# A Fourier filter on half the spectrum, folded a second time: quarter-length transforms and a batch build spread over the FFN

## The chip, the cores and the metric

The kernel runs on one core of one Trainium2 chip. The number that counts is device time in microseconds (us) of one execution. Engines of the core work side by side, each through its own list of instructions in a fixed order: TensorE (PE, with its weight loads shown apart as PEld), VectorE (DVE), ScalarE (ACT), GpSimd (POOL, which here starts the loads) and SyncE (SP, which starts the stores). TensorE's clock has two levels, 1.2 and 2.4 GHz; a profile shows the share of the upper one that was granted.

## The reference

Two parts, one after the other. For each of 8 batches of 3008 positions by 256 channels a real Fourier transform along the positions, a product with a complex filter (1505 frequencies by 256 channels), and the inverse transform. Then, on the 24064 rows that come out, a gated feed-forward network (FFN):

```python
X = np.fft.rfft(x, axis=1)                       # x: 8 x 3008 x 256
y = np.fft.irfft(X * (filt_r + 1j*filt_i)[None], n=3008, axis=1)
x = y.reshape(24064, 256)
out = (np.maximum(x @ w_gate, 0.0) * (x @ w_val)) @ w_out   # 256 -> 1536 -> 256
```

## The kernel before

The transforms are matrix products. A real transform of 3008 positions needs cosines and sines of 3008 x 1505 angles; the kernel first folds position n with position 3008-n, so that sum and difference of 1505 positions remain, and one square table each of cosines (`G_c`) and sines (`G_s`), 1505 x 1505 in 16 bits, serves forward and inverse.

Stages:

- `build_uv(b)` (L255 on) makes the folded input of a batch in 12 chunks of up to 128 positions: POOL loads the chunk `xa` and its mirror `xm` (L265, L269), PE reverses the mirror with a permutation matrix (`xrev`, L271), ACT copies it out of PSUM (L278), DVE writes sum and difference into `uv` (L279, L281).
- `gen_acs` and `gen_stripe` make the tables in six column stripes of 256. Stripe 0 comes from angles on DVE and `Sin` on ACT (L185 to L208); the others from stripe 0 by a rotation on PE: DVE builds three diagonal matrices `dg` (L217), four products of 256 columns go into `gen_s` and `gen_c`, ACT copies them out (L230, L231).
- `forward_chunk` makes 128 frequencies: 12 products of 256 columns into `xr_ps` (L299), 12 into `xi_ps` (L306); ACT scales both out of PSUM (L313, L315); six operations of DVE multiply by the filter into `yf` (L318 to L324).
- `inverse_batch` makes, per half of the channels (2) and per tile of 512, 512 and 481 positions, 12 products into `p_ps` (L338) and 12 into `q_ps` (L345); ACT copies `q_ps` (L352), DVE writes p-q and p+q to the two mirrored places of `y` (L353, L359).
- `ffn_batch` goes through 8 windows of 384 positions (the last has 320). Per window 12 blocks of gate and value, four products each (`g_ps` L376, `v_ps` L383), a copy on ACT (`ge`, L389) and the gated product on DVE (`h`, L390); then 36 products into `o_ps` (L398), a copy and a store.

All PSUM tiles come from one pool of eight banks used in turn. Two batches are built ahead of everything else (`n_pre` = 2); the tables are made stripe by stripe, and after each stripe both batches' forward chunks of those columns run. From then on, in the order of the program: for batch b the forward transform (if b is 2 or more), the build of batch b+2, the inverse, the FFN:

```python
        nb = b + n_pre
        if nb < B:
            uv_tiles[nb] = build_uv(nb)
        y = inverse_batch(b, yf_tiles.pop(b))
        ffn_batch(b, y)
```

A framework orders each engine's list when the program is built (`tc.high_priority()` moves a block forward) and adds the semaphore waits; when the kernel runs, each engine takes its list strictly in turn.

Of the kernel before, what the change touches and what calls it, by code (L numbers as in the profile page):

```python
# [19 lines left out]
def kernel(  # L20
# [10 lines left out]
    nc = tc.nc  # L31
# [4 lines left out]
    NF = S // 2 + 1  # L36
    Dff = moe_w_gate.shape[1]
# [36 lines left out]
    xload = ctx.enter_context(tc.tile_pool(name="xload", bufs=3))  # L74
# [20 lines left out]
    nc.vector.tensor_add(wvec, wvec, wvec_tmp)
    nc.vector.tensor_scalar(out=wvec, in0=wvec, scalar1=-1.0 / N, scalar2=2.0 / N,
                            op0=ALU.mult, op1=ALU.add)
    wvec_neg = const.tile([P, nM], FP32)
    nc.vector.tensor_scalar_mul(wvec_neg, wvec, -1.0)

    lastc = nM - 1
    rows_last = msz(lastc)
    hi_last = rows_last - 1 if (lastc * P + rows_last - 1) == NF - 1 else rows_last
    cond_last = hi_last - 1
# [6 lines left out]
                            op0=ALU.is_equal)  # L111
    if cond_last != P - 1:
# [13 lines left out]
    G_c = gmat.tile([P, nM, NF], FP16)  # L126
    G_s = gmat.tile([P, nM, NF], FP16)

    MAGIC = float(2 ** 23)
    two_pi = 2.0 * math.pi  # L130

    nDer = nGW - 1
    if nDer > 0:
        acs = const.tile([P, nM, nDer, 3], FP32)

    def gen_acs():
        if nDer == 0:
            return
        colk = gen.tile([P, nDer], FP32, tag="colk", bufs=1)
        nc.gpsimd.iota(colk, [[GW, nDer]], base=GW, channel_multiplier=0,  # L140
                       allow_small_or_imprecise_dtypes=True)
        for mi in range(nM):
            rows = msz(mi)
            ph = gen.tile([P, 2, nDer], FP32, tag="acs_ph")
            nc.vector.tensor_scalar(
                out=ph[:rows, 0, :], in0=colk[:rows, :],
                scalar1=rowval_n[:rows, mi:mi + 1], scalar2=None, op0=ALU.mult)
            nc.vector.tensor_scalar(
                out=ph[:rows, 1, :], in0=ph[:rows, 0, :],
                scalar1=0.25, scalar2=None, op0=ALU.add)  # L150
            rnd = gen.tile([P, 2, nDer], FP32, tag="acs_rn")
            nc.vector.tensor_scalar(
                out=rnd[:rows, 0, :], in0=ph[:rows, 0, :],
                scalar1=MAGIC, scalar2=MAGIC, op0=ALU.add, op1=ALU.subtract)
            nc.vector.tensor_scalar(
                out=rnd[:rows, 1, :], in0=ph[:rows, 1, :],
                scalar1=MAGIC, scalar2=MAGIC, op0=ALU.add, op1=ALU.subtract)
            red = gen.tile([P, 2, nDer], FP32, tag="acs_rd")
            nc.vector.scalar_tensor_tensor(
                out=red[:rows, 0, :], in0=rnd[:rows, 0, :], scalar=-1.0,  # L160
                in1=ph[:rows, 0, :], op0=ALU.mult, op1=ALU.add)
            nc.vector.scalar_tensor_tensor(
                out=red[:rows, 1, :], in0=rnd[:rows, 1, :], scalar=-1.0,
                in1=ph[:rows, 1, :], op0=ALU.mult, op1=ALU.add)
            nc.scalar.activation(
                out=acs[:rows, mi, :, 1], in_=red[:rows, 0, :],
                func=AF.Sin, scale=two_pi)
            nc.scalar.activation(
                out=acs[:rows, mi, :, 0], in_=red[:rows, 1, :],
                func=AF.Sin, scale=two_pi)  # L170
            nc.vector.tensor_scalar(
                out=acs[:rows, mi, :, 2], in0=acs[:rows, mi, :, 1],
                scalar1=-1.0, scalar2=None, op0=ALU.mult)

    def gen_stripe(gj):
        cols = gwsz(gj)
        c0 = gj * GW
        if gj == 0:
            colv = gen.tile([P, GW], FP32, tag="colv", bufs=1)
            nc.gpsimd.iota(colv[:, :cols], [[1, cols]], base=c0, channel_multiplier=0,  # L180
                           allow_small_or_imprecise_dtypes=True)
            for mi in range(nM):
                rows = msz(mi)
                phi = gen.tile([P, 2, GW], FP32, tag="phi", bufs=1)
                nc.vector.tensor_scalar(  # L185
                    out=phi[:rows, 0, :cols], in0=colv[:rows, :cols],
                    scalar1=rowval_n[:rows, mi:mi + 1], scalar2=None, op0=ALU.mult)
                nc.vector.tensor_scalar(
                    out=phi[:rows, 1, :cols], in0=phi[:rows, 0, :cols],
                    scalar1=0.25, scalar2=None, op0=ALU.add)  # L190
# [48 lines left out]
    def load_weights():  # L239
# [230 lines left out]
```

## Time and profile before

| what | value |
|---|---|
| time, median of 4 runs (lowest to highest) | 1445.79 us (1443.77 to 1448.33) |
| the profiled execution's own time | 1445.38 us |
| its span in the profile | 1443.6 us |
| PE busy | 1319.0 us, 91% of the span, 9168 products |
| DVE, ACT, POOL busy | 49%, 43%, 9% |
| mean granted clock | 0.975 |

The span runs from the first to the last instruction that the profile shows; the other 1.8 us of that execution lie around it. "Busy" of DVE and ACT adds up durations, and neighbouring instructions overlap, so what an instruction occupies is read from the distance of two starts in the timeline. The chain of waits names, going back from the last instruction, what each step waited for; its PE pieces give the rate at which products really follow each other.

### The profile page before, as it was taken

How to read it: one execution, taken by the hardware profiler on the slowest of the kernel's cores; microseconds unless marked ns; L12 is line 12 of the kernel's file. 1: busy time of each engine (PE TensorE's matmuls, PEld its weight loads, DVE VectorE, ACT ScalarE, POOL GpSimd, SP SyncE). 2: the span in 40 equal slices, each digit the busy share in tenths (PEclk: the TensorE clock that was granted, in tenths of full speed). 3: DMA queues.
4: the chain of work that ended last, by engine and by line, in shares of the span. 5: the costliest groups of instructions: out<-in, count | busy, mean ns of one | idle time of the engine just before them, and what ended most of it. 6: DMA issues, size and time to landing. Idle time of an engine off the chain costs nothing.

```text
span 1443.6 us, 24775 instructions
## 1 busy us (share of the span) xinstructions
PE 1319.0 (91%) x9168; PEld 897.8 (62%) x9168; DVE 707.8 (49%) x1977; ACT 626.7 (43%) x1466; POOL 124.4 (9%) x241
## 2 busy tenths in 40 slices
PE   2179989988999799997999899997999999999999
PEld 0047736663677557784577746775577856776666
DVE  2486635552554435543455525554355435553455
ACT  2255524551554225542355315542255415542455
POOL 6700030012000300003000120002000000000000
PEclk9999989998999899998999989998999999999999
DMA  8700030122010301103011120102011000100011
GB/s 115 91 1 1 1 43 23 34 45 31 25 35 29 44 0 34 37 18 43 12 37 38 16 30 26 38 26 32 1 34 37 19 1 26 35 27 1 19 35 35
DMA packets 60248, 42.46 MB, mean 29 GB/s; under 512 B 6942, under 2 KB 59616, under 8 KB 60128
## 3 DMA queue, kind: packets, MB, share of 16 engines
q0 software_dynamic: 32992, 16.24, 9.4%
q1 hardware_dynamic: 27136, 24.65, 5.1%
q8 instruction: 71, 1.16, 0.3%
q14 instruction: 49, 0.40, 0.1%
HBM read 32.44 MB, written 24.64 MB: 40 GB/s over the span
## 4 chain that ended last, share of the span: by engine, by line
PE 63%; issue 29%; POOL 4%; DMA 3%; DVE 1%; ACT 0%; POOLq 0%; DVEq 0%; ACTq 0%
PE o_ps L398 13%; PE g_ps L376 13%; PE v_ps L383 13%; PE p_ps L338 7%; PE q_ps L345 6%; PE xr_ps L299 5%; PE xi_ps L306 5%; DMA xm<-in_x_dram 2%; POOL xm L269 2%; POOL xa L265 1%; DMA xa<-in_x_dram 1%; POOL filt_r_sb L251 0%; POOL w_out_sb L246 0%; POOL filt_i_sb L251 0%; PE xrev L271 0%
## 5 line engine op out<-in xcount | busy, mean ns | idle before, releaser
L390 DVE SCALAR_TENSOR_TENSOR h<-ge,v_ps 128x384 f16<-128x384 f16 (+1 forms) x768 | 409.9, 545 | 290.5 <-ACT ge L389 199.4
L389 ACT CAST ge<-g_ps 128x384 f16<-128x384 f32 (+1 forms) x768 | 360.0, 472 | 110.0 <-PE g_ps L376 78.1
L376 PE MATMUL g_ps<-y,w_gate_sb 128*128 128x384 f16 (+1 forms) x1536 | 370.2, 323 | 0.0
L383 PE MATMUL v_ps<-y,w_val_sb 128*128 128x384 f16 (+1 forms) x1536 | 370.2, 323 | 0.0
L398 PE MATMUL o_ps<-w_out_sb,h 128*128 128x256 f16 (+1 forms) x2304 | 263.0, 273 | 0.0
L398 PEld LDWEIGHTS <-h 128*128 128x128 f16 (+1 forms) x2304 | 225.8, 98 | 33.2 <-issue 1.7
L383 PEld LDWEIGHTS <-w_val_sb 128*128 128x128 f16 x1536 | 150.2, 98 | 94.2
L376 PEld LDWEIGHTS <-w_gate_sb 128*128 128x128 f16 x1536 | 150.3, 98 | 89.3
L299 PE MATMUL xr_ps<-uv,G_c 128*128 128x256 f16 (+3 forms) x1152 | 145.0, 274 | 26.7 <-ACT G_c L208 26.7
L404 ACT COPY ob<-o_ps 128x256 f32<-128x256 f32 x192 | 71.4, 372 | 204.6 <-PE o_ps L398 185.7
L306 PE MATMUL xi_ps<-uv,G_s 128*128 128x256 f16 (+3 forms) x1152 | 146.4, 274 | 5.9 <-ACT G_s L205 5.9
L338 PE MATMUL p_ps<-G_c,yf 128*128 128x512 f16 (+1 forms) x576 | 141.5, 398 | 0.0
L299 PEld LDWEIGHTS <-G_c 128*128 128x128 f16 (+3 forms) x1152 | 113.2, 100 | 41.8 <-ACT G_c L208 27.2
L345 PE MATMUL q_ps<-G_s,yf 128*128 128x512 f16 (+1 forms) x576 | 130.3, 375 | 0.0
L353 DVE TENSOR_TENSOR y<-p_ps,qs 128x512 f16<-128x512 f32 (+1 forms) x48 | 32.7, 682 | 196.3 <-ACT qs L352 196.3
L269 POOL DMA_DIRECT2D xm<-in_x_dram x96 | 52.8, 562 | 869.2 <-PE xrev L271 865.7
L352 ACT CAST qs<-q_ps 128x512 f16<-128x512 f32 (+1 forms) x48 | 27.7, 578 | 229.7 <-PE q_ps L345 229.7
L306 PEld LDWEIGHTS <-G_s 128*128 128x128 f16 (+3 forms) x1152 | 113.6, 100 | 21.5 <-ACT G_s L205 9.1
L338 PEld LDWEIGHTS <-yf 128*128 128x128 f16 x576 | 59.3, 103 | 73.1 <-issue 12.3
L345 PEld LDWEIGHTS <-yf 128*128 128x128 f16 x576 | 56.1, 97 | 67.0 <-issue 1.1
L271 PE MATMUL xrev<-xm,J_mid 128*128 128x256 f16 (+1 forms) x88 | 28.7, 352 | 75.1 <-DMA xm<-in_x_dram 74.1
L313 ACT ACTIVATE xt<-xr_ps,wvec 128x256 f16<-128x256 f32 x96 | 45.3, 473 | 82.8 <-PE xr_ps L299 77.0
(68 smaller groups left out, 650.2 us busy)
## 6 DMA issues: line engine op xcount, KB each, us to landing
out_dram<-ob SPq DMA_DIRECT2D x184, 128.0 KB, 1.7
xa<-in_x_dram POOLq DMA_DIRECT2D x88, 64.0 KB, 2.5
xm<-in_x_dram POOLq DMA_DIRECT2D x80, 64.0 KB, 2.5
w_gate_sb<-in_moe_w_gate_dram POOLq DMA_DIRECT2D x2, 384.0 KB, 6.5
w_val_sb<-in_moe_w_val_dram POOLq DMA_DIRECT2D x2, 384.0 KB, 5.7
w_out_sb<-in_moe_w_out_dram POOLq DMA_DIRECT2D x12, 64.0 KB, 2.7
filt_r_sb<-in_filt_r_dram POOLq DMA_DIRECT2D x11, 64.0 KB, 3.1
filt_i_sb<-in_filt_i_dram POOLq DMA_DIRECT2D x11, 64.0 KB, 3.3
```

Source lines behind the costliest of these rows:

```text
L269: nc.gpsimd.dma_start(xm16[:R, :], x[b, r0:r0 + R, :])
L299: nc.tensor.matmul(xr_ps[:F, :D], lhsT=G_c[:rows, sc, f0:f0 + F], rhs=uv[:rows, sc, 0, :], start=(sc == 0), stop=(sc == nM - 1))
L306: nc.tensor.matmul(xi_ps[:F, :D], lhsT=G_s[:rows, sc, f0:f0 + F], rhs=uv[:rows, sc, 1, :], start=(sc == 0), stop=(sc == nM - 1))
L313: nc.scalar.activation(out=xt[:F, 0, :], in_=xr_ps[:F, :D], func=AF.Copy, scale=wvec[:F, fc:fc + 1])
L338: nc.tensor.matmul(p_ps[:dn, :L], lhsT=yf[:F, fc, 0, d0:d0 + dn], rhs=G_c[:F, fc, t0:t0 + L], start=(fc == 0), stop=(fc == nM - 1))
L345: nc.tensor.matmul(q_ps[:dn, :L], lhsT=yf[:F, fc, 1, d0:d0 + dn], rhs=G_s[:F, fc, t0:t0 + L], start=(fc == 0), stop=(fc == nM - 1))
L376: nc.tensor.matmul(g_ps[:Fn, :L], lhsT=w_gate_sb[:dn, dc, fc * P:fc * P + Fn], rhs=y[:dn, dc, t0:t0 + L], start=(dc == 0), stop=(dc == nDC ...
L383: nc.tensor.matmul(v_ps[:Fn, :L], lhsT=w_val_sb[:dn, dc, fc * P:fc * P + Fn], rhs=y[:dn, dc, t0:t0 + L], start=(dc == 0), stop=(dc == nDC ...
L389: nc.scalar.copy(ge[:Fn, :L], g_ps[:Fn, :L])
L390: nc.vector.scalar_tensor_tensor(out=h[:Fn, fc, :L], in0=ge[:Fn, :L], scalar=0.0, in1=v_ps[:Fn, :L], op0=ALU.max, op1=ALU.mult)
L398: nc.tensor.matmul(o_ps[:gn, :D], lhsT=h[:Fn, fc, g0:g0 + gn], rhs=w_out_sb[:Fn, fc, :], start=(fc == 0), stop=(fc == nFF - 1))
L404: nc.scalar.copy(ob[:gn, :], o_ps[:gn, :D])
```

## The change

The input is folded twice. Positions n, 3008-n, 1504+n and 1504-n are combined, so that even and odd frequencies part: 753 even and 752 odd ones, each over 753 positions. Four components per position stand in `uv`. Three pairs of tables replace the one: `G2` (even frequencies, both directions, 753 x 753), `AoF` (odd, forward) and `AoI` (odd, inverse), each in three column stripes in place of six, from 18 angle blocks and 36 rotated blocks (before 12 and 60).

- `build_uv`: 6 chunks; per chunk four loads, two reversals, and eight operations of DVE, four of which read the reversal in PSUM (the copy on ACT goes). For the first two batches the angles of `G2` and `AoF` stripe 0 are made inside it. The pool of its buffers goes from three to two.
- `forward_chunk`: 12 chunks as before, each with 6+6 products in place of 12+12. What ACT and DVE do per chunk is the same.
- `inverse_batch`: tiles of 512 and 241 positions; 4 x 6 products per tile; two copies on ACT; four operations of DVE out of PSUM into `cb`, four from `cb` to the four places of `y`.
- `ffn_batch`: as before, and after each of its first six windows one chunk of the build of batch b+2.
- The order of loads at the start and the constants of the angles (`colk`, `colv`, `colvo`) ahead of them; the filter is loaded by every second row.

The driver: the forward chunks come in pairs of even and odd, and the build is handed to the FFN.

```diff
+            for (par, fc) in fwd_chunks(0, nM2):
+                forward_chunk(b, uv, yf_tiles[b], par, fc)
...
-        if nb < B:
-            uv_tiles[nb] = build_uv(nb)
         y = inverse_batch(b, yf_tiles.pop(b))
-        ffn_batch(b, y)
+        ffn_batch(b, y, nb if nb < B else None)
```

`ffn_batch`, at the end of a window (`per` is 1 here):

```diff
+            if nb is not None:
+                per = _ceil_div(nM2, nFW - 1)
+                cs = [c for c in range(tw * per, tw * per + per) if c < nM2]
+                uv_tiles[nb] = build_uv(nb, uv_tiles.get(nb), cs)
```

`build_uv`, per chunk; of the four operations that read `revB` or `revC` and of the four that write `uv`, one each stands here:

```diff
+            xa16 = xload.tile([P, 2, D], FP16, tag="xa16")
+            nc.gpsimd.dma_start(xa16[:rows, 0, :], x[b, s0:s0 + rows, :])
+            nc.gpsimd.dma_start(xa16[:rows, 1, :], x[b, NH + s0:NH + s0 + rows, :])
...
-                    nc.scalar.copy(xr16[:rows, :], xrev[:rows, :D])
...
+                    nc.vector.tensor_add(w[:rows, 0, :], xa16[:rows, 0, :],
+                                         revB[:rows, :D])
...
+                    nc.vector.tensor_add(uv[:rows, mi, 0, :], w[:rows, 0, :],
+                                         w[:rows, 2, :])
```

`forward_chunk`: the two chains of products are half as long (`nM2` is 6, `nM` was 12).

```diff
-        for sc in range(nM):
-            rows = msz(sc)
+        for sc in range(nM2):
+            rows = m2sz(sc)
             nc.tensor.matmul(
                 xr_ps[:F, :D],
-                lhsT=G_c[:rows, sc, f0:f0 + F],
-                rhs=uv[:rows, sc, 0, :],
+                lhsT=mat_c[:rows, sc, f0:f0 + F],
+                rhs=uv[:rows, sc, ucomp, :],
```

`inverse_batch`, per tile, behind six products each into `pe`, `qe`, `po` and `qo`; three more operations of the last form write the places NH-t (backwards), NH+t and N-t (backwards) of `y`, with t the position, NH = 1504, N = 3008:

```diff
+                    nc.scalar.copy(ev[:dn, 0, :L], qe[:dn, :L])
+                    nc.scalar.copy(ev[:dn, 1, :L], qo[:dn, :L])
+                    nc.vector.tensor_sub(cb[:dn, 0, :L], pe[:dn, :L], ev[:dn, 0, :L])
+                    nc.vector.tensor_add(cb[:dn, 1, :L], pe[:dn, :L], ev[:dn, 0, :L])
+                    nc.vector.tensor_sub(cb[:dn, 2, :L], po[:dn, :L], ev[:dn, 1, :L])
+                    nc.vector.tensor_add(cb[:dn, 3, :L], po[:dn, :L], ev[:dn, 1, :L])
+                    nc.vector.tensor_add(y[:dn, dc, t0:t0 + L], cb[:dn, 0, :L],
+                                         cb[:dn, 2, :L])
```

Where this moves instructions, in three places. First PE between the forward transform of batch 2 and its inverse, before: 12 reversals (`xrev`) of the mirrored loads `xm` of batch 4, one behind the other, stand between the last `xi_ps` and the first `p_ps`.

```order
L306 MATMUL xi_ps<-uv_2293,G_s 97x256
L271 LDWEIGHTS J_mid
L271 MATMUL xrev<-xm_5857,J_mid 128x256
...
L271 MATMUL xrev<-xm_5957,J_mid 128x256
L271 LDWEIGHTS J_last
L271 MATMUL xrev<-xm_5967,J_last 97x256
L338 LDWEIGHTS yf_5409
L338 MATMUL p_ps<-G_c,yf_5409 128x512
```

Now PE has one pair of reversals (`revB`, `revC`) behind the `o_ps` products of each of the first six windows of an FFN, here the first window of batch 0.

```order
L525 MATMUL o_ps<-w_out_sb,h 128x256
L338 LDWEIGHTS J_mid
L338 MATMUL revB<-xm_2174,J_mid 128x256
L341 LDWEIGHTS J_mid
L341 MATMUL revC<-xm_2174,J_mid 128x256
L503 LDWEIGHTS w_gate_sb
L503 MATMUL g_ps<-y_1852,w_gate_sb 128x384
```

The row of twelve reversals has moved out of the space between forward and inverse; two at a time stand between the windows of the FFN.

Second, DVE at the end of an inverse transform, before: the last two tiles of a batch's `y` (here of batch 4), two operations out of PSUM each, and then the gated products of all FFN windows.

```order
L353 TENSOR_TENSOR y_7978<-p_ps,qs 128x512
L359 TENSOR_TENSOR y_7978<-p_ps,qs 128x512
L353 TENSOR_TENSOR y_7978<-p_ps,qs 128x481
L359 TENSOR_TENSOR y_7978<-p_ps,qs 128x480
L390 SCALAR_TENSOR_TENSOR h<-ge,v_ps 128x384 x84
```

Now DVE goes through this for the last tiles of batch 0 (`cb` holds the four sums and differences of a tile), then through the gated products of the first FFN window, then through the first chunk of the next build (`w`, `uv`).

```order
L464 TENSOR_TENSOR y_1852<-cb 128x512
L470 TENSOR_TENSOR y_1852<-cb 128x512
L462 TENSOR_TENSOR cb<-po,ev 128x241
L463 TENSOR_TENSOR cb<-po,ev 128x241
L464 TENSOR_TENSOR y_1852<-cb 128x241
L470 TENSOR_TENSOR y_1852<-cb 128x240
L478 TENSOR_TENSOR y_1852<-cb 128x511
...
L486 TENSOR_TENSOR y_1852<-cb 128x511
L517 SCALAR_TENSOR_TENSOR h<-ge,v_ps 128x384 x12
L345 TENSOR_TENSOR w<-xa_2171,revB 128x256
...
L359 TENSOR_TENSOR uv_2170<-w 128x256
```

Ten operations stand between the last tile's `cb<-pe` and the first `h`, where there were two; eight of a build stand between two windows, where there were none.

Third, POOL at the start, before: the last loads of batch 1 (`xm_356`, `xa_354`), then the weights' last part and the filter, then the column constant `colk`.

```order
L269 DMA xm_356<-in_x_dram 96x256
L265 DMA xa_354<-in_x_dram 97x256
L246 DMA w_out_sb<-in_moe_w_out_dram 128x256 x11
L251 DMA filt_r_sb<-in_filt_r_dram 128x256 x11
L251 DMA filt_r_sb<-in_filt_r_dram 97x256
L251 DMA filt_i_sb<-in_filt_i_dram 128x256 x11
L251 DMA filt_i_sb<-in_filt_i_dram 97x256
L140 IOTA colk 128x5
```

Now `colk` is ahead of the first load, and the last load of x for batch 1 (`xa_478`) stands among the last of the filter.

```order
L199 IOTA colk 128x2
L202 IOTA colv 128x256
L205 IOTA colvo 128x256
L329 DMA xa_146<-in_x_dram 128x256
...
L308 DMA filt_sb<-in_filt_i_dram 128x256
L329 DMA xa_478<-in_x_dram 113x256
L330 DMA xa_478<-in_x_dram 113x256
L308 DMA filt_sb<-in_filt_i_dram 128x256 x4
L308 DMA filt_sb<-in_filt_i_dram 112x256
```

The constants have moved ahead of everything, the last load of x behind most of the weights.

## Rows read from the trace of the kernel before

**Rows 1.** The page, part 1: busy us (share of the span) xinstructions of each engine.

```profile
PE 1319.0 (91%) x9168; PEld 897.8 (62%) x9168; DVE 707.8 (49%) x1977; ACT 626.7 (43%) x1466; POOL 124.4 (9%) x241
```

**Rows 2.** Busy time by stretch: forward, inverse, FFN of batch 6, then all of batch 7.

```profile
core 0: us, PE busy (x) PEld busy (x) DVE busy (x) ACT busy (x) POOL busy (x), PEclk, DMA share, GB/s
1130.42:1162.07 31.65, 31.65 (x289) 28.50 (x290) 15.81 (x68) 11.26 (x24) 0.00 (x0) 1.00 0.02 7
1162.07:1192.70 30.63, 30.63 (x146) 14.03 (x145) 7.29 (x14) 3.38 (x6) 0.00 (x0) 1.00 0.00 1
1192.70:1285.34 92.64, 92.64 (x673) 65.65 (x672) 52.22 (x98) 53.28 (x120) 0.00 (x0) 1.00 0.10 33
1285.34:1440.30 154.96, 154.92 (x1104) 108.10 (x1104) 75.47 (x180) 68.03 (x150) 0.00 (x0) 1.00 0.06 21
```

**Rows 3.** The same view: two of the six stretches with a build.

```profile
187.00:200.00 13.00, 8.64 (x29) 3.24 (x30) 4.15 (x18) 3.24 (x9) 9.83 (x19) 0.62 0.79 92
487.40:502.00 14.60, 6.49 (x19) 2.19 (x18) 6.19 (x28) 4.30 (x13) 12.75 (x24) 0.61 0.86 97
```

**Rows 4.** Waits: who waited for whom: us in total, times, longest us.

```profile
PE xrev L271 <- DMA xm<-in_x_dram: 79.3, 62, 5.3
DVE ph L145 <- POOL colk L140: 16.5, 1, 16.5
```

**Rows 5.** The chain of waits: start us, us, what; twelve products, and the last piece.

```profile
1162.07 2.60 PE p_ps L338 x12
...
1288.07 1.31 PE xr_ps L299 x12
...
1436.21 4.06 PE o_ps L398 x36
```

**Rows 6.** Timeline of DVE, end of a forward transform and inverse: start us, us, what.

```profile
1157.57 0.28 DVE L323 TENSOR_TENSOR m<-xt,filt_r_sb 128x256 f16<-128x256 f16 x1
1157.77 0.28 DVE L320 TENSOR_TENSOR yf<-m 128x256 f16<-128x256 f16 x1
...
1183.26 0.69 DVE L353 TENSOR_TENSOR y<-p_ps,qs 128x512 f16<-128x512 f32 x1 [4.00 <-ACT qs L352]
1183.87 0.68 DVE L359 TENSOR_TENSOR y<-p_ps,qs 128x511 f16<-128x511 f32 x1
```

**Rows 7.** Timelines of PE, DVE and ACT, batch 6, first FFN window.

```profile
1192.50 0.49 PE L376 MATMUL g_ps<-y,w_gate_sb 128*128 128x384 f16 x2
...
1194.48 5.63 DVE L390 SCALAR_TENSOR_TENSOR h<-ge,v_ps 128x384 f16<-128x384 f16 x10
...
1195.11 0.94 ACT L389 CAST ge<-g_ps 128x384 f16<-128x384 f32 x2 [0.96 <-DVE h L390]
1196.26 0.95 ACT L389 CAST ge<-g_ps 128x384 f16<-128x384 f32 x2 [0.21 <-PE g_ps L376]
```

**Rows 8.** Timelines of PE and DVE, batch 6, second FFN window.

```profile
1204.23 0.49 PE L376 MATMUL g_ps<-y,w_gate_sb 128*128 128x384 f16 x2
...
1205.26 7.71 DVE L390 SCALAR_TENSOR_TENSOR h<-ge,v_ps 128x384 f16<-128x384 f16 x12 [4.01 <-ACT ge L389]
...
1212.03 4.09 PE L398 MATMUL o_ps<-w_out_sb,h 128*128 128x256 f16 x36
```

**Rows 9.** Busy time by stretch: first loads; stripes 1 to 5 with their forward chunks.

```profile
0.00:60.00 60.00, 9.31 (x24) 2.61 (x24) 13.31 (x59) 11.43 (x26) 48.09 (x98) 1.00 0.92 115
89.30:187.00 97.70, 86.81 (x726) 68.31 (x724) 65.07 (x324) 56.68 (x171) 2.86 (x6) 0.98 0.02 3
```

**Rows 10.** Timeline of ACT: rotation factors (`acs`), then the angle blocks.

```profile
62.25 0.21 ACT L165 ACTIVATE acs<-red 128x5 f32<-128x5 f32 x1 [0.28 <-DVE red L159]
...
62.85 0.21 ACT L165 ACTIVATE acs<-red 128x5 f32<-128x5 f32 x1 [0.25 <-DVE red L162]
...
69.94 0.42 ACT L205 ACTIVATE G_s<-red 128x256 f16<-128x256 f32 x1 [1.11 <-DVE red L199]
...
71.80 0.42 ACT L205 ACTIVATE G_s<-red 128x256 f16<-128x256 f32 x1 [1.11 <-DVE red L199]
```

**Rows 11.** Timelines of DVE and PE: diagonal matrices; one stripe's rotated blocks.

```profile
97.64 4.50 DVE L217 TENSOR_SCALAR dg<-ident,acs 128x128 f16<-128x128 f16 x23 [0.27 <-PE gen_c L228]
...
130.01 0.27 PE L221 MATMUL gen_s<-G_c,dg 128*128 128x256 f16 x1
...
137.47 0.71 PE L299 MATMUL xr_ps<-uv,G_c 128*128 128x256 f16 x5
```

More of the change, by code (lines that the diff above doesn't have):

```diff
@@ L36 @@
     NF = S // 2 + 1
+    NH = S // 2
+    NQ = S // 4
+    M2 = NQ + 1
+    MO = NQ
     Dff = moe_w_gate.shape[1]
@@ L138, in gen_acs @@
             return
[L139 to L184, printed above, removed]
+        for fam in range(3):
+            nch = nM2 if fam != 2 else nMO
+            for mi in range(nch):
+                rows = m2sz(mi) if fam != 2 else mosz(mi)
+                if fam == 0:
+                    rscale = row_n2[:rows, mi:mi + 1]
+                elif fam == 1:
+                    rscale = row_n2[:rows, mi:mi + 1]
+                else:
+                    rscale = rowodd_n[:rows, mi:mi + 1]
+                ph = gen.tile([P, 2, nDer], FP32, tag="acs_ph")
@@ L185, in gen_stripe @@
                 nc.vector.tensor_scalar(
[L186 to L187 removed]
+                    out=ph[:rows, 0, :], in0=colk[:rows, :],
+                    scalar1=rscale, scalar2=None, op0=ALU.mult)
                 nc.vector.tensor_scalar(
[L189 removed]
+                    out=ph[:rows, 1, :], in0=ph[:rows, 0, :],
@@ L233 @@
+            for mi in range(nMO):
+                rows = mosz(mi)
+                _derived_blocks(AoI_c, AoI_s, mi, rows,
+                                acs[:rows, 2, mi, k, 0:1], acs[:rows, 2, mi, k, 1:2],
+                                acs[:rows, 2, mi, k, 2:3], ce, c0)
     w_gate_sb = wts.tile([P, nDC, Dff], FP16)
@@ L258, in build_uv @@
+    n_pre = min(2, B)
+    def build_uv(b, uv=None, chunks=None):
+        if uv is None:
+            uv = uvp.tile([P, nM2, 4, D], FP16, tag="uv", name=f"uv{b}")
+        for mi in (range(nM2) if chunks is None else chunks):
+            if b < n_pre:
+                sine_block(b, mi)
+            rows = m2sz(mi)
             s0 = mi * P
             lo = 1 if mi == 0 else 0
-            hi = rows - 1 if (s0 + rows - 1) == NF - 1 else rows
+            is_last = (s0 + rows - 1) == NQ
+            hi = rows - 1 if is_last else rows
@@ new lines, in build_uv @@
+                xm16 = xload.tile([P, 2, D], FP16, tag="xm16")
+                rB = N - s0 - hi + 1
+                nc.gpsimd.dma_start(xm16[:R, 0, :], x[b, rB:rB + R, :])
+                rC = NH - s0 - hi + 1
+                nc.gpsimd.dma_start(xm16[:R, 1, :], x[b, rC:rC + R, :])
+                revB = psum.tile([P, TW], FP32, tag="ps", name="revB")
+                nc.tensor.matmul(revB[:rows, :D], lhsT=J[:R, :rows],
+                                 rhs=xm16[:R, 0, :], start=True, stop=True)
@@ new lines, in inverse_batch @@
+                qe = psum.tile([P, TW], FP32, tag="ps", name="qe")
+                qo = psum.tile([P, TW], FP32, tag="ps", name="qo")
+                for fc in range(nM2):
+                    F = m2sz(fc)
+                    nc.tensor.matmul(
+                        pe[:dn, :L], lhsT=yf[:F, 0, fc, 0, d0:d0 + dn],
+                        rhs=G2_c[:F, fc, t0:t0 + L],
+                        start=(fc == 0), stop=(fc == nM2 - 1))
+                for fc in range(nM2):
+                    F = m2sz(fc)
+                    nc.tensor.matmul(
+                        qe[:dn, :L], lhsT=yf[:F, 0, fc, 1, d0:d0 + dn],
+                        rhs=G2_s[:F, fc, t0:t0 + L],
+                        start=(fc == 0), stop=(fc == nM2 - 1))
```

383 lines of the change are left out of this document (248 added, 135 removed).

## The prediction

> **What bounds the kernel now.** I read the busy totals first, then busy time by stretch, the chain of waits, the waits, and the timelines of PE and DVE where stages meet. PE is busy for 91% of the span, no other engine for half of it [rows 1]. Busy time does not show whether PE is the limit at every moment; the stretches do. In the forward transform, the inverse and the FFN of batch 6 PE is busy throughout at the full granted clock, while DVE has work for half the time or less [rows 2]. The chain of waits gives PE's rate: twelve products of 256 columns take 1.31 us (0.1095 each), twelve of 512 columns 2.60 us (0.2167) [rows 5]. So a product less is time less there. In two kinds of places PE is not the limit: the six builds of batches 2 to 7, in which it waits for loads (about 13 us each, PE busy for 6.5 of 14.6 us in one, mean granted clock 0.61) [rows 3, 4], and the start, up to 187 us, where loads, angles and rotated tables come one behind the other [rows 9].
>
> As a check of the method: 187 for the start, six builds at 13, two batches without forward (124 each, one of them a little cold), six with it (154.9 each) and 3.3 us behind the last `o_ps` (1436.21 + 4.06 to the span's end, 1443.6) [rows 2, 3, 5] make 187 + 78 + 248 + 929.5 + 3.3 = 1446, against a span of 1443.6.
>
> **Transforms.** Forward: 12 chunks of 12 products per batch in place of 24: 144 x 0.1095 = 15.8 us for 31.65 [rows 2, 5]. Inverse: per half of the channels 24 products of 512 columns (5.20) and 24 of 241 columns. No row has 241; between the two rates it is 0.103, so 2.47, and the inverse is 2 x 7.67 = 15.3 us for 30.63. That holds if DVE and ACT keep up. Per forward chunk PE now takes 1.31 us, and DVE's six operations start 0.20 us apart [rows 6], 1.23 us: it keeps up, barely. Per tile of 512 positions of the inverse DVE reads PSUM four times at 0.61 us from start to start [rows 6] and makes four 16-bit operations on SBUF. No row has those at 512 columns. If they go like the filter's (256 columns in 0.205, where 512 out of PSUM take 0.61, so two elements go in the time of one) they take 0.34; at the PSUM rate 0.61. With 241 columns by the same lines (0.33, and 0.20 or 0.33) DVE needs 5.9 us per half, at worst 7.5, against PE's 7.67. It keeps up, and what costs is the tail.
>
> At the end E of the last product DVE still has two PSUM operations of 241 columns, the two first sums of 512, and six more into `y`: about 3.0 us, so the first `h` of the FFN starts at E + 3.0 where it normally starts 1.03 us behind the first `g_ps` [rows 8]. Queued behind it are all `h`, and PE waits for those, since the eight PSUM banks let it run four blocks ahead (2.6 us). Before, the first window also began late, `h` at 1.98 us, caught up at 0.58 us per block against PE's 0.65, and PE lost nothing [rows 7]. Two us late instead of 0.95 costs about 0.6 us at the fifth block and 0.3 at the first `o_ps`: I take 1.0 per batch; ends 0 (as in rows 7) and 3 (PSUM rate, nothing caught up).
>
> **Builds.** The twelve reversals between forward and inverse go, and with them six waits of 13 us, 78 us in all. What is late next? Loads of chunk i+2 wait only for the use of chunk i, one window of 11.7 us (1204.23 to 1212.03, and 36 products at 0.109) earlier [rows 8], so I count no wait for loads. Two reversals cost PE 0.22 us per window. But DVE makes eight operations between the reversals and the next `h`: four out of PSUM of 256 columns (0.34 each, on the line through 0.61), four at 0.205, together 2.2 us. The first `h` then starts 2.4 us behind the first `g_ps` instead of 1.03 [rows 8]. It is 1.4 late; the fifth block's bank comes 0.1 late; twelve blocks at 0.58 win back 0.8; the last `h` comes 0.25 late for the first `o_ps`. So 0.35 per window plus 0.22: 3.4 us per FFN with a build, for six FFNs (36 windows). Ends: 0.22, all hidden as in rows 7, and 1.6, nothing won back.
>
> **Start.** POOL needed 60 us for 98 instructions, with the DMA engines 92% busy, and the bytes are the same [rows 9]. The last load of x moves behind most weights, so the folded input of batch 1 comes at 57 + 2.5 to land + 2.3 on DVE = 62 us. (DVE's own work until then: twelve angle blocks at 1.86, twelve builds at 2.2, eight filter chunks at 1.23, 59 us [rows 6, 10]; I see 58 to 75.) Then: the rest of batch 1's first four chunks, 6; rotation factors, 18 x 0.59, 10.6, which before could not start until `colk` came [rows 4, 10]; stripe 1 on DVE, six angle blocks (11.0) and 54 diagonals at 0.196 (10.6) [rows 10, 11], 21.6; eight forward chunks, 10.5; stripe 2, 18 blocks at 0.62 (7.46 us for twelve) [rows 11] and 1.6 to begin, 12.8; eight chunks, 10.5. Sum 134 us, for 187; ends 118 (DVE and PE overlap in stripe 1, no stalls in the loads) and 155.
>
> **Sum.** 134 + two batches without forward and with a build, 15.3 + 1.0 + 92.64 + 3.4 = 112.4 each + four with both, 128.2 each + two without a build, 124.8 each + 3.3 = 134 + 224.8 + 512.8 + 249.6 + 3.3 = 1124.5 us of span. The profiled execution took 1445.38 for its span of 1443.6, and the median of the runs is 0.4 above it: 1124.5 + 1.8 + 0.4 = 1126.7, so 1127.
>
> **What the Trainium skill would make of it.** DVE's starts lie 0.20 us apart where an operation lasts 0.28 [rows 6]. The Trainium skill, "VectorE: DVE Perf Modes", section "The DRAIN you can't avoid", says that the next operation does not start until the pipeline has emptied; by that rule the trace does not agree, since here it starts before the one ahead has ended. The rule would make the filter of a chunk last 6 x 0.28 = 1.7 us, more than PE's 1.31, which is the second rival below. The same page, "Mode 2x_1P", asks for 4-byte alignment for the double rate; the places NH+t of `y` begin at odd elements, and the skill's "Vector Engine (DVE) Microarchitecture Reference", section 5.1, finds alignment to make no difference and calls negative steps unmeasured. No row of before has either; by the first the tail at E would be about 1.2 us longer per batch, 10 us in all.
>
> **Rivals.**
> 1. The start is not shortened: with two buffers per kind in place of three, POOL, DVE and PE wait for each other in turn, and the later loads, the weights among them, shift. For it: POOL's list is strictly in order, and its loads of x now wait on DVE between angle blocks. Against: DVE's 59 us of work fit beside 60 us of loads. Start at 155: 1148.
> 2. DVE by full durations: forward chunks 1.7 us, 12 x 0.39 = 4.7 us more in six batches (28), a build 2.8 instead of 2.2 us (36 x 0.6 = 22), tails 1 us (8). 1127 + 58 = 1185. Against it stand the starts in rows 6.
> 3. The builds cost more: each `h` late by 1.4 us is never won back, 36 x 1.25 more, and tails at 3: 1127 + 45 + 16 = 1188; with half of it 1157. Against it rows 7.
> 4. Nothing waits: start 118, no tails, builds at 0.22: 1127 - 16 - 8 - 13 = 1090.
> 5. Slower. The new waits of PE, at 36 windows and eight inverses, let TensorE's clock fall, as in a build of before (mean 0.61 of full) [rows 3], and the FFN then runs at 1.2 GHz. PE's work behind the start is about 8 x 108 + 6 x 15.8 = 960 us at the full rate; at half the rate it takes twice as long, so above a third of it (320 us) the kernel is slower than before; with half of it 1127 + 480 = 1600. Against: a window that began with `h` 0.95 us late kept a clock of 1.00 [rows 2, 7].
>
> That the change does less than it says can be left out: PE's list has 7536 products for 9168, and the missing ones are those of the two transforms and of the tables.
>
> **How the numbers follow.** Forecast 0.62 (1100 to 1148), rival 1 0.12, rival 2 0.05, rival 3 0.12 (1150 to 1190), rival 4 0.06, rival 5 0.02; 0.01 for no change. Range 1097 to 1166: the forecast, rival 1, half of rival 3, half of rival 4. Faster by over 0.2% (3 us, about what a measurement can tell) 0.97, within it 0.01, slower 0.02.
>
> **What would show it.** In the profile after: six products of 256 columns in 0.66 us and of 512 in 1.30 on the chain; a forward of 15.8 and an inverse of 15.3 us with PE busy throughout; no wait of a reversal for a load behind the start; the first `h` 3.0 us behind the last inverse product and 2.4 behind the first `g_ps` of a window with a build, with at most half a us of idle PE; the first inverse product at 134 us. Wrong would be: PE waiting for `yf` at the start of an inverse, idle gaps of over 1 us per window, a clock below 0.95 behind the start, or a start above 155.

## The result and the profile after

The changed kernel takes 1111.4 us (median of 8 runs, 1110.22 to 1112.62) where the kernel before takes 1445.8: ratio 0.7688, 95% interval 0.7681 to 0.7696, or 334 us less. 1127 was predicted. The profiled execution took 1112.62 for a span of 1110.9.

The page, part 1, beside [rows 1]:

```profile
PE 1044.3 (94%) x7536; PEld 736.2 (66%) x7536; DVE 773.4 (70%) x2337; ACT 581.2 (52%) x1361; POOL 125.5 (11%) x242
```

PE lost 275 us of work; DVE, which had gained work, is now busy for 70% and PE for 94%: PE waits less, though the engine beside it is closer to full. The stretches beside [rows 2], with the same columns: forward, inverse and FFN with a build (batch 2), then an FFN without a build (batch 6):

```profile
350.82:366.76 15.94, 15.94 (x146) 14.41 (x146) 13.92 (x66) 10.27 (x24) 0.00 (x0) 1.00 0.04 10
366.76:382.10 15.34, 15.34 (x98) 9.30 (x96) 10.36 (x29) 3.81 (x8) 0.00 (x0) 1.00 0.00 1
382.10:477.43 95.33, 95.16 (x686) 66.30 (x685) 64.29 (x155) 53.55 (x120) 12.73 (x24) 1.00 0.23 48
889.00:982.50 93.50, 93.33 (x674) 65.60 (x673) 53.95 (x107) 53.10 (x120) 0.00 (x0) 1.00 0.09 32
```

Forward and inverse are half as long as in [rows 2], PE is busy throughout, and the clock is at its upper level in all four. DVE is busy for 13.92 of 15.94 us of a forward transform: it keeps up with little to spare. (Such a row counts overlapped time once, since 66 operations of 0.28 us would add up to 18.5; it is not the sum of durations that the section on the profile before calls it.) On the chain of waits (start, us, what) six products stand where [rows 5] have twelve, at the same time for one:

```profile
351.59 0.66 PE xi_ps L393 x6
...
366.76 1.30 PE pe L433 x6
```

One window of the FFN with a build, PE, then DVE and ACT (start us, us, engine, line, operation):

```profile
406.54 0.27 PE L338 MATMUL revB<-xm,J_mid 128*128 128x256 f16 x1
406.65 0.27 PE L341 MATMUL revC<-xm,J_mid 128*128 128x256 f16 x1
406.76 0.49 PE L503 MATMUL g_ps<-y,w_gate_sb 128*128 128x384 f16 x2
...
410.01 0.49 PE L503 MATMUL g_ps<-y,w_gate_sb 128*128 128x384 f16 x2
410.34 0.49 PE L510 MATMUL v_ps<-y,w_val_sb 128*128 128x384 f16 x2
...
414.56 4.18 PE L525 MATMUL o_ps<-w_out_sb,h 128*128 128x256 f16 x36
...
406.85 0.42 DVE L345 TENSOR_TENSOR w<-xa,revB 128x256 f16<-128x256 f16 x1 [3.11 <-PE revB L338]
...
408.99 6.78 DVE L517 SCALAR_TENSOR_TENSOR h<-ge,v_ps 128x384 f16<-128x384 f16 x12
409.63 0.95 ACT L516 CAST ge<-g_ps 128x384 f16<-128x384 f32 x2 [1.22 <-DVE h L517]
```

The first `h` starts 2.23 us behind the first `g_ps` (1.03 in [rows 8]), yet PE goes from the reversals to `o_ps` without a gap: 7.80 us for twelve blocks. The ACT row is the third copy `ge`: with two buffers for `ge`, it waits for the first `h`. The PE rows at 410.01 and 410.34 are the sixth block, the first that needs banks which the first `h` and this copy set free. The reversals wait for no load. From one first `o_ps` to the next it is 12.03 us (402.53 to 414.56) where a window without a build takes 11.73: 0.22 for the reversals, 0.08 because the `o_ps` products run 4.18 us in place of 4.09.

The end of an inverse, DVE and then PE:

```profile
382.18 0.42 DVE L464 TENSOR_TENSOR y<-cb 128x512 f16<-128x512 f16 x1
382.51 0.42 DVE L470 TENSOR_TENSOR y<-cb 128x512 f16<-128x512 f16 x1
382.84 0.41 DVE L462 TENSOR_TENSOR cb<-po,ev 128x241 f16<-128x241 f32 x1
...
383.86 0.62 DVE L478 TENSOR_TENSOR y<-cb 128x511 f16<-128x511 f16 x2
384.39 0.62 DVE L486 TENSOR_TENSOR y<-cb 128x240 f16<-128x240 f16 x2
384.92 6.32 DVE L517 SCALAR_TENSOR_TENSOR h<-ge,v_ps 128x384 f16<-128x384 f16 x11
...
385.08 0.49 PE L510 MATMUL v_ps<-y,w_val_sb 128*128 128x384 f16 x2
385.53 0.48 PE L503 MATMUL g_ps<-y,w_gate_sb 128*128 128x384 f16 x2
386.09 0.49 PE L510 MATMUL v_ps<-y,w_val_sb 128*128 128x384 f16 x2
...
390.31 4.36 PE L525 MATMUL o_ps<-w_out_sb,h 128*128 128x256 f16 x36
```

The last inverse product ends at 382.03, the first `h` starts 2.9 us later, and PE shows two small gaps around the `g_ps` of the sixth block (0.45 and 0.56 from start to start instead of 0.33). The first `o_ps` products behind it take 4.36 us, where 4.09 are usual [rows 8].

The start, beside [rows 9], and the longest wait of PE in it:

```profile
0.00:60.00 60.00, 22.20 (x106) 12.20 (x107) 50.37 (x200) 13.89 (x34) 52.37 (x105) 0.97 0.98 121
60.00:97.00 37.00, 14.52 (x84) 8.22 (x81) 35.22 (x245) 23.69 (x90) 0.99 (x2) 0.63 0.07 9
97.00:129.40 32.40, 31.27 (x269) 25.86 (x270) 28.75 (x145) 24.39 (x71) 0.00 (x0) 1.00 0.00 2
```
```profile
PE gen_s L182 <- DVE dg L177: 22.0, 5, 16.9
```

Three limits one behind the other: transfers up to 60 us (DMA 98% busy), DVE from 60 to 97 (35.2 of 37 us, PE at a granted clock of 0.63, near its lower level), PE from there. The first inverse product starts at 129.2. Before, it started at 194.35, behind the first of the six builds, whose reversals began at 183.57:

```profile
183.57 0.49 PE L271 MATMUL xrev<-xm,J_mid 127*128 127x256 f16 x3
...
194.35 4.05 PE L338 MATMUL p_ps<-G_c,yf 128*128 128x512 f16 x12
```

The prediction's border of 187 us between the start and the builds lies inside that build.

Counted with that border, the 334 us come, to within about 2 us, from six forward transforms (15.7 each, 94), eight inverses (15.3 each, 122), the start (58) and six builds (13 each against 1.8 in the windows, 67), less eight tails of 0.86 (7). With the border at 183.57 the start is worth 54 and the builds 70.

### The profile page after: what moved, and what is told of

Read it like the earlier page. It is cut to its first block, busy times and chain, and to the rows that moved or that the text cites. A ratio compares the mean times of both kernels' runs of the same rounds, so it can differ in the third digit from the quotient of the medians.

```text
span 1110.9 us, 21588 instructions
## 1 busy us (share of the span) xinstructions
PE 1044.3 (94%) x7536; PEld 736.2 (66%) x7536; DVE 773.4 (70%) x2337; ACT 581.2 (52%) x1361; POOL 125.5 (11%) x242
## 4 chain that ended last, share of the span: by engine, by line
PE 85%; DVE 7%; POOL 3%; ACT 2%; issue 1%; DMA 1%; ACTq 0%; DVEq 0%; POOLq 0%
PE o_ps L525 22%; PE v_ps L510 21%; PE g_ps L503 21%; PE xr_ps L386 5%; PE xi_ps L393 5%; PE qo L451 2%; PE pe L433 2%; PE qe L439 2%; PE po L445 2%; POOL filt_sb L308 1%; ACT ge L516 1%; DVE h L517 1%; DVE cb L463 1%; PE gen_s L182 1%; DMA w_val_sb<-in_moe_w_val_dram 1%
## 5 line engine op out<-in xcount | busy, mean ns | idle before, releaser
L334 POOL DMA_DIRECT2D xm<-in_x_dram x48 | 25.9, 540 | 671.2 <-PE revC L341 668.9
L411 DVE TENSOR_TENSOR m<-xt,filt_sb 128x256 f16<-128x256 f16 (+1 forms) x96 | 27.4, 285 | 30.5 <-ACT xt L406 30.0
L386 PE MATMUL xr_ps<-uv,G_c 128*128 128x256 f16 (+3 forms) x288 | 41.0, 278 | 4.2 <-DVE w L347 2.5
L386 PE MATMUL xr_ps<-uv,AoF_c 128*128 128x256 f16 (+3 forms) x288 | 40.7, 276 | 2.4 <-DVE w L347 1.2
L393 PE MATMUL xi_ps<-uv,AoF_s 128*128 128x256 f16 (+3 forms) x288 | 40.6, 275 | 1.2 <-ACT AoF_s L166 1.0
L393 PE MATMUL xi_ps<-uv,G_s 128*128 128x256 f16 (+3 forms) x288 | 40.7, 276 | 0.0
L433 PE MATMUL pe<-G_c,yf 128*128 128x512 f16 (+1 forms) x192 | 36.0, 323 | 0.0
L439 PE MATMUL qe<-G_s,yf 128*128 128x512 f16 (+1 forms) x192 | 36.0, 323 | 0.0
L451 PE MATMUL qo<-AoI_s,yf 128*128 128x512 f16 (+1 forms) x192 | 36.0, 323 | 0.0
L445 PE MATMUL po<-AoI_c,yf 128*128 128x512 f16 (+1 forms) x192 | 36.0, 323 | 0.0
## 6 DMA issues: line engine op xcount, KB each, us to landing
xm<-in_x_dram POOLq DMA_DIRECT2D x16, 63.5 KB, 2.5
```

The source lines that it names most:

```text
L386: nc.tensor.matmul(xr_ps[:F, :D], lhsT=mat_c[:rows, sc, f0:f0 + F], rhs=uv[:rows, sc, ucomp, :], start=(sc == 0), stop=(sc == nM2 - 1))
L393: nc.tensor.matmul(xi_ps[:F, :D], lhsT=mat_s[:rows, sc, f0:f0 + F], rhs=uv[:rows, sc, vcomp, :], start=(sc == 0), stop=(sc == nM2 - 1))
L433: nc.tensor.matmul(pe[:dn, :L], lhsT=yf[:F, 0, fc, 0, d0:d0 + dn], rhs=G2_c[:F, fc, t0:t0 + L], start=(fc == 0), stop=(fc == nM2 - 1))
L439: nc.tensor.matmul(qe[:dn, :L], lhsT=yf[:F, 0, fc, 1, d0:d0 + dn], rhs=G2_s[:F, fc, t0:t0 + L], start=(fc == 0), stop=(fc == nM2 - 1))
L445: nc.tensor.matmul(po[:dn, :L], lhsT=yf[:F, 1, fc, 0, d0:d0 + dn], rhs=AoI_c[:F, fc, t0:t0 + L], start=(fc == 0), stop=(fc == nMO - 1))
L451: nc.tensor.matmul(qo[:dn, :L], lhsT=yf[:F, 1, fc, 1, d0:d0 + dn], rhs=AoI_s[:F, fc, t0:t0 + L], start=(fc == 0), stop=(fc == nMO - 1))
```

## The experiments

All medians stand beside about 1446 us for the kernel before in the same runs (1445.8 to 1447.0).

**The build put back between forward and inverse.**

```diff
+        if nb < B:
+            uv_tiles[nb] = build_uv(nb)
         y = inverse_batch(b, yf_tiles.pop(b))
-        ffn_batch(b, y, nb if nb < B else None)
+        ffn_batch(b, y)
```

> The changed kernel with one thing undone: the build of batch b+2 again stands as one block between forward transform and inverse. Theory (the builds were waits of PE for loads, and the FFN hides them): two of six chunks are loaded ahead, the other four (1.03 MB as written, at the 92 to 97 GB/s of rows 3) take about 11 us, with the landing of the first about 12.5; the windows give back 0.30 us x 6 = 1.8. So 6 x 10.7 = 64 more: 1175 us (1160 to 1190), with PE waiting for xm for about 60 us behind the start and a granted clock near 0.6 there. Rival (with twelve reversals in place of... six pairs, a build costs little wherever it stands, and the gain is the fold's alone): 1111 to 1120.

Measured: 1174.9 us (ratio 0.8125, 0.8112 to 0.8139), 63.5 more. The build made before the inverse of batch 1, that inverse, and the largest wait behind the start:

```profile
248.38:258.26 9.88, 3.06 (x13) 1.27 (x13) 8.52 (x31) 0.37 (x1) 6.76 (x13) 0.77 0.73 98
258.26:274.85 16.59, 16.59 (x97) 9.66 (x96) 13.57 (x40) 3.44 (x7) 6.01 (x12) 0.93 0.42 46
```
```profile
PE revB L338 <- DMA xm<-in_x_dram: 33.6, 14, 5.6
```

This build holds PE for 9.9 us with 3 us of work, at a mean clock of 0.77, and the inverse behind it takes 16.6 us in place of 15.3. With the 1.8 us that the windows no longer pay, that is 9.4 us for the batch. The total came as the theory had it, the parts not: all six builds hold PE for 62.6 us, but of these it is at work for 20, and the waits for `xm` are 38 (34 at `revB`, 4 at `revC`) instead of some 60. The mean clock in the six is between 0.62 and 0.81.

**The build alone spread, in the kernel before.** `build_uv` takes the chunks as an argument, and `ffn_batch` calls it:

```diff
+            if nb is not None and 2 * tw < nM:
+                uv_tiles[nb] = build_uv(nb, uv_tiles.get(nb), [2 * tw, 2 * tw + 1])
```

> The kernel before, with only the build spread: two of its twelve chunks behind each of the first six FFN windows, tables and transforms as before. Theory: six waits of 13 us go, and a window pays 0.22 us for two reversals and next to nothing for two copies on ACT and four 16-bit operations on DVE, 1.5 us per FFN: 1446 - 6 x 11.5 = 1377 us (1370 to 1385). Fold and spread then add up: 1446 - 1377 = 69 here, 64 in the run with the build put back, and the fold alone about 266. Rival (loads in the FFN collide with the stores, or wait for buffers): the gain is under 40 us, 1406 or more.

Measured: 1375.6 us (0.9517, 0.9503 to 0.9531), 70.3 less. Behind the start no wait of PE is left; the first 73 us from there on:

```profile
187.00:260.00 73.00, 72.90 (x455) 44.08 (x453) 34.86 (x72) 30.98 (x70) 6.35 (x12) 1.00 0.15 28
```

So fold and spread nearly add up: the spread is worth 70.3 alone and 63.5 on top of the fold, the fold alone 271, and 70.3 + 271 is 7 more than both together.

**The `o_ps` chains in reverse order.**

```diff
-                for fc in range(nFF):
+                for fc in range(nFF - 1, -1, -1):
...
-                        start=(fc == 0), stop=(fc == nFF - 1))
+                        start=(fc == nFF - 1), stop=(fc == 0))
```

> The changed kernel with the twelve products of each o_ps chain taken in the reverse order, last h block first. Theory (PE hides the late last h because the first o_ps chain reads h block by block and comes to the last one only after eleven products, 1.2 us): now PE must wait for the last h, which ends about 0.95 us behind the last v_ps product in a plain window and about 1.2 in one with a build: 28 x 0.95 + 36 x 1.2 = 70 us more, 1180 (1160 to 1190). Rival, as the prediction's step had it (the first o_ps chain needs the last h when it starts, in either order): 1111 to 1116.

Measured: 1184.4 us (0.8193, 0.8179 to 0.8206), 73.0 more. The one wait of PE behind the start, and one of its 64 places:

```profile
PE o_ps L525 <- DVE h L517: 66.6, 64, 1.3
```
```profile
410.33 4.10 PE L525 MATMUL o_ps<-w_out_sb,h 128*128 128x256 f16 x36 [1.29 <-DVE h L517]
```

The last `h` is about a microsecond late in every window, of the kernel before too (it ends at 1212.97, `o_ps` begins at 1212.03 [rows 8]). In forward order eleven products cover it; taken first, it costs 1.14 us per window. Two windows with a build, then two without, in the chain of waits of this run:

```profile
559.54 4.10 PE o_ps L525 x36
...
572.77 4.11 PE o_ps L525 x36
...
954.45 4.10 PE o_ps L525 x36
...
967.19 4.11 PE o_ps L525 x36
```

With the order reversed a window takes 13.23 us with a build and 12.74 without, where the changed kernel takes 12.03 and 11.73. So the order hides about 1.0 us in every window, and of the price of a build only 0.2: 0.49 in place of 0.30.

**The four writes of `uv` done twice, in the FFN alone.**

```diff
+                    for _ in range(2 if b >= n_pre else 1):
                         nc.vector.tensor_add(uv[:rows, mi, 0, :], w[:rows, 0, :],
```

> The changed kernel with the four operations that write uv done twice in each chunk that is built inside an FFN: 4 x 0.205 = 0.82 us more on DVE per window with a build. Theory (the v_ps of the fifth block needs the bank that the first h frees; it comes 2.92 us behind the first g_ps, and the first h now ends at 2.77, so 0.15 us are to spare and beyond that each us of DVE costs one): 0.67 at the fifth block and about 0.1 at the first o_ps chain, 0.8 x 36 = 28 us more: 1139 (1131 to 1144). Rival (lateness is won back in the window at 0.085 us per block, ACT and DVE being faster than PE): under 3 us, 1111 to 1114.

Measured: 1140.3 us (0.7888, 0.7877 to 0.79), 28.9 more, 0.80 per window. PE at the fifth and sixth block, with DVE and ACT:

```profile
418.93 0.49 PE L511 MATMUL v_ps<-y,w_val_sb 128*128 128x384 f16 x2
419.04 3.33 DVE L518 SCALAR_TENSOR_TENSOR h<-ge,v_ps 128x384 f16<-128x384 f16 x6
419.64 0.48 PE L504 MATMUL g_ps<-y,w_gate_sb 128*128 128x384 f16 x2 [0.23 <-DVE h L518]
419.68 0.94 ACT L517 CAST ge<-g_ps 128x384 f16<-128x384 f32 x2 [2.02 <-DVE h L518]
420.21 0.48 PE L511 MATMUL v_ps<-y,w_val_sb 128*128 128x384 f16 x2
...
424.43 4.36 PE L526 MATMUL o_ps<-w_out_sb,h 128*128 128x256 f16 x36
```

The size is as expected, the place is one block further. The fifth block (its `v_ps` at 418.93) runs before the first `h` begins, so it needs nothing from it; of the eight banks only those of the first two `g_ps`, which ACT has copied by then, can be free. So the banks are not used strictly in turn, as the section on the kernel before has it. The sixth block waits, its `g_ps` for the first `h`, its `v_ps` (420.21) for the third `ge` behind it: 0.71 and 0.57 us from start to start instead of 0.33, 0.62 lost. The other 0.18 is lost in the first `o_ps` products (4.36 us for 4.18). The changed kernel sits near the edge: 0.82 us more on DVE cost 0.80.

**The start: buffers, rotation factors, one batch ahead.** Three buffers for loads (`bufs=3` in place of 2 for `xload`):

> The changed kernel with three buffers per kind for the loads of x, as before the change, in place of two. Theory (up to 60 us the start is bound by the transfers themselves, the DMA engines being busy 98% of that time, and from there to 97 us by DVE): no change, 1111 (1108 to 1114). Rival (rival 1 of the prediction: two buffers make POOL, DVE and PE wait for each other): the loads end earlier, 1095 to 1107.

Measured: 1109.2 us (0.7675, 0.7662 to 0.7688), 2.2 less. That lies inside the theory's range, and the interval overlaps that of the changed kernel, so in the time the gain is hardly clear. The first 60 us:

```profile
0.00:60.00 60.00, 17.36 (x74) 9.00 (x75) 53.51 (x241) 15.63 (x44) 56.13 (x110) 1.00 1.00 126
```

DVE gets 3 us more done under the loads (53.5 against 50.4), and the first inverse product starts at 125.6, 3.6 earlier. In the profile, then, the two buffers did hold DVE back a little, and the transfers alone were not quite the limit.

Rotation factors made at once:

```diff
+        for k in range(nDer):
+            nc.vector.tensor_scalar_mul(ph[:, 0, 0, :, k], row_n2, float(GW * (k + 1)))
+            nc.vector.tensor_scalar_mul(ph[:, 0, 1, :, k], rowodd_n, float(GW * (k + 1)))
...
+            nc.scalar.activation(out=acs[:, f, :, :, 1], in_=red[:, 0, f],
+                                 func=AF.Sin, scale=two_pi)
```

> The changed kernel with the rotation factors made for all chunks at once: about ten small operations of DVE and four Sin on ACT in place of 18 groups of seven and two (the factors of G2 and AoF are the same numbers, so two sets are made, not three). In the changed kernel they take 10.4 us, 66.3 to 76.7, alone on DVE, with PE idle. Theory (from 60 to 97 us DVE's list is the path): some 2 us remain, so 8 to 9 less: 1103 (1101 to 1106). Rival (PE, at a granted clock of 0.63 there, or ACT with the angles of AoI takes over as the bound): under 3 less, 1108 or more.

Measured: 1103.4 us (0.7634, 0.7622 to 0.7645), 8.0 less; the first inverse product starts at 120.2.

One batch ahead (`n_pre = 1`, the loads of the filter ahead of the FFN's weights, and in the build of batch 0):

```diff
-            if b < n_pre:
-                sine_block(b, mi)
+            if b == 0:
+                sine_block(0, mi)
+                sine_block(1, mi)
```

> The changed kernel with one batch built ahead of the tables instead of two: the angles of G2 and AoF are both made in the build of batch 0, batch 1 is built inside the FFN of batch 0 (seven such FFNs), and the filter is loaded ahead of the FFN's weights. Theory (the start is a sum of loads, 60 us for two batches and all weights, and DVE work): x of batch 0 (3.1 MB at the 115 to 127 GB/s of the start) takes 27 us, but DVE needs 12 x 1.86 + 6 x 2.2 = 36 us beside it, then four filter chunks 5, factors 10.6, stripe 1 21.6, chunks 5, stripe 2 12.8, chunks 5: the first inverse product at 96 us in place of 129.4. Batch 1's forward transform (15.94) now comes behind the start, with six more windows with a build (1.8): 1111 - 33.4 + 17.7 = 1096 (1088 to 1103). Rival (loads set the start's length whatever is moved, the weights last at 95 us, and the FFN or DVE waits for them): 1108 or more.

Measured: 1093.2 us (0.7563, 0.7552 to 0.7574), 18.2 less; the first inverse product starts at 92.7.

```profile
0.00:30.00 30.00, 12.64 (x44) 5.28 (x44) 28.37 (x116) 7.87 (x18) 28.95 (x60) 1.00 0.90 102
30.00:60.00 30.00, 7.52 (x28) 2.51 (x28) 29.73 (x207) 16.92 (x67) 11.91 (x23) 1.00 0.66 98
```

DVE is busy for 58 of the first 60 us: it is the path, and the loads are not.

Both edits together:

> Both of the two edits, one batch ahead and the factors made at once. Theory (DVE bounds the start from its first load on): the gains add up, 1096 - 8.5 = 1087 (1079 to 1095). Rival (with one batch ahead the start is bound by loads, the filter's above all): no less than with one batch ahead alone, 1094 or more.

Measured: 1084.0 us (0.7498, 0.7487 to 0.7509), 9.3 below one batch ahead alone. The gains add up, and this is the fastest version here, 27 us below the changed kernel.

With that, the third diagonal of each rotated block on ACT:

```diff
-        nc.vector.tensor_scalar(out=dg[:rows, 2, :rows], in0=ident[:rows, :rows],
-                                scalar1=ph_sn, scalar2=None, op0=ALU.mult)
+        nc.scalar.activation(out=dg[:rows, 2, :rows], in_=ident[:rows, :rows],
+                             func=AF.Copy, scale=ph_sn)
```

> One batch ahead, factors made at once, and the third of the three diagonal matrices of each rotated block made on ACT instead of DVE (36 of 108). Theory (DVE is the path only up to the end of stripe 1; in the run with the first two edits DVE is busy 28.9 of 30 us from 30 to 60 us, and PE 9.0 to 10 of each 10 us from there on): stripe 1's 18 diagonals at 0.196 go from the path, 3.5 us, those of stripe 2 lie beside PE: 1084 - 3.5 = 1080.5 (1078 to 1082.5). Rivals: DVE is the path through both stripes, 36 x 0.196 = 7 less, 1077; or the diagonals on ACT queue behind its copies and sines and PE waits for them instead, 1084 or more.

Measured: 1088.4 us (0.7521, 0.7508 to 0.7533), 4.4 more (3.3 if each is set against the kernel before that ran beside it), and the first inverse product starts at 88.2 instead of 82.7: the theory falls, the second rival holds. ACT in stripe 2, first without the edit, then with it:

```profile
70.73 0.38 ACT L191 CAST AoF_s<-gen_s 128x240 f16<-128x240 f32 x1
...
71.83 0.38 ACT L191 CAST AoF_s<-gen_s 128x240 f16<-128x240 f32 x1
```
```profile
71.85 0.38 ACT L191 CAST AoF_s<-gen_s 128x240 f16<-128x240 f32 x1
72.10 0.39 ACT L192 CAST AoF_c<-gen_c 128x240 f16<-128x240 f32 x1
72.35 0.43 ACT L179 ACTIVATE dg<-ident,acs 128x128 f16<-128x128 f16 x1
72.66 0.38 ACT L191 CAST G_s<-gen_s 128x241 f16<-128x241 f32 x1
72.90 0.44 ACT L179 ACTIVATE dg<-ident,acs 128x128 f16<-128x128 f16 x1
...
73.44 0.41 ACT L191 CAST AoF_s<-gen_s 128x240 f16<-128x240 f32 x1
```

Two blocks took 1.10 us on ACT; with two diagonals more, at 0.30 from start to start, they take 1.59, and in these rows ACT has no idle time left. DVE gave away only 0.165 us per diagonal (starts at 87.23, 87.39, 87.56 and 87.72 in the changed kernel; the 0.196 that the prediction takes from [rows 11] is the average of a group with pauses), and ACT, which copies every block out of PSUM, became the path.

> The same with three buffers per kind for the loads of x. Theory (with one batch ahead DVE is busy 28 of the first 30 us, so a third buffer has no idle time of DVE to fill): no change against the run without it, 1080.5 (within 1.5). Rival (the third buffer lets the loads of batch 0 end earlier and the filter with them, as the 2 us with two batches ahead suggest): 2 to 4 less.

Measured: 1090.2 us (0.7533, 0.7522 to 0.7544), 1.8 above the run without it, with intervals that overlap. No gain, as the theory said; whether the loss is real stays open.

## Why the prediction was right, and where it was off

The path was right in every stage. Two terms of the sum were too large, and in one of them, the price of a build in a window, the mechanism failed too.

**Transforms.** Forward 15.94 (15.8 predicted), inverse 15.34 (15.3), both at PE's rate. Rival 2, DVE by full durations, falls: a forward transform would have taken 12 x 1.7 = 20.4 us. The Trainium skill, "VectorE: DVE Perf Modes", section "The DRAIN you can't avoid", gives that rule; by its own pointer to "Two Vector instructions with no wait between them", a next operation that is not held starts earlier, and the trace agrees with that sentence: 0.20 us from start to start at 0.28 each [rows 6].

**Tails.** First `h` at 2.9 us behind the last inverse product (3.0 predicted), cost 0.86 per batch (93.50 against 92.64 in [rows 2]; 1.0 predicted). Of it 0.35 lies at the sixth block (0.6 predicted, at the fifth), 0.27 in the first `o_ps` products (0.3 predicted), and 0.1 in where the two stretches were cut (0.20 and 0.09 us behind the first `g_ps`). The reverse and odd places of `y` cost nothing extra: 0.33 us per 512 columns, forwards and backwards, and 0.53 for 511 from an odd place and 241 more (383.86 to 384.39; 0.33 and 0.20 at the prediction's rates); the 10 us that the prediction worked out for odd places did not come.

**Builds: the term that was mis-sized.** 0.57 us per window was predicted, 0.30 measured, over 36 windows 9.7 of the 15.3 us between forecast and result. The step that failed is the 0.35 us that PE was to lose to DVE's delay: "the fifth block's bank comes 0.1 late" and "the last `h` comes 0.25 late for the first `o_ps`". In their place 0.08 was measured. DVE's side was about right: the first `h` starts 2.23 us behind the first `g_ps` (2.4 predicted), and the last ends 1.21 behind the start of `o_ps`, where without a build it ends 0.94 behind [rows 8], so 0.27 later. (That this figure came so close is luck: the prediction's own terms, 1.4 late, 0.1 lost and 0.8 won back, leave 0.5 and not 0.25.) What it had wrong is when PE needs these results. First, PE runs five blocks ahead, not four. The sixth block's `v_ps` starts at 410.34, and the copy that frees its bank ends at 410.11 (409.63 and 0.48, half of two), so about 0.2 us were to spare, as the doubled writes bear out (0.82 added, 0.62 lost there). Second, the first `o_ps` chain takes the `h` blocks in turn and needs the last one only after eleven products, 1.2 us in. With the chain reversed, which takes that cover away, a build costs 0.49 us per window: the 0.22 of the reversals and 0.27, about the 0.25 that was predicted. Rival 3 (1.25 more per window) falls with this; of rival 4 the price of a build (0.22) was nearer than the forecast's, but its start of 118 and its free tails did not come.

**Start.** 129.2 us for 134, 4.8 of the difference in the span. Batch 1's input and its first chunks were done at 66.3 instead of 68, the factors took 10.4 (10.6 predicted), stripe 1 about 20.8 (21.6), and the forward chunks with stripe 2 took 31.7 (33.8). Small excesses in one direction, then; in stripe 1 the diagonals were priced at 0.196 instead of 0.165, 1.7 us for 54. Rival 1 (the start not shortened, because of two buffers) falls: a third buffer is worth 2 us, not 21.

**Sum.** In the span: start 4.8, two batches without forward 3.2, four with it 5.9 (forward was 0.14 longer than predicted), less 0.3 that the last two batches and the end took longer: 13.6 = 1124.5 - 1110.9. The other 1.7 us lie between span and median, where 2.2 were added and 0.5 was right.

**Rival 5**, the clock falling in the FFN, falls: 1.00 in every stretch behind the start. Where PE has 3 us of work in 10, as in the build put back, the clock is at 0.77; the small gaps of the changed kernel don't show in it.

## What to carry to other kernels

A block of work that waits for loads is worth spreading over a stage in which another engine's lead hides it; how much fits is read from two places, when the first late result frees the buffer that the leading engine needs, and when the last one is consumed, in the order of consumption. Here about 0.2 us were left at the first place: of 0.82 us more work on DVE 0.62 was lost there and 0.18 at the second. At a start made of several limits in series, cut the engine that the stretch's own row shows as full (DVE here, 27 us in two edits), and look at the row of the engine that is to take work over before moving it there.

## What the runs showed of the hardware

- DVE's 16-bit operations on SBUF wrote 512 columns in 0.33 us whether they ran forwards (382.18) or backwards (382.51), and no more where they began at an odd element (383.86); out of PSUM the same width took 0.61 [rows 6]. The Trainium skill, "Vector Engine (DVE) Microarchitecture Reference", section 5.1, finds that alignment makes no difference, and the trace agrees; for negative steps, which it lists as not measured, these rows show the same rate.
- Scaling a 128 x 128 matrix by a value per row took 0.30 us from start to start on ACT, between copies, and 0.165 on DVE.
- Behind ten microseconds with little PE work the inverse was slower: in the run with the build put back, PE had 3.06 us of work from 248.38 to 258.26 us at a mean granted clock of 0.77, and the inverse from there to 274.85 ran at 0.93 and took 16.6 us instead of 15.3.
